# Two-branch attention on one core: another order at the end, one group turned by TensorE, and the first chunk's sums turned two slots later

## The chip, the cores and the metric

The kernel runs on one core of a Trainium2 chip. The core has TensorE (PE, matmuls into PSUM), ScalarE (ACT), VectorE (DVE), GpSimd (POOL) and SyncE (SP), which here only issues DMAs. Each engine works through its own queue in order, and semaphores make one wait for another. The metric is the device time of one execution in microseconds, the median of several.

## The reference

Two attention layers over 2048 tokens of 640 features, 32 heads of 20, whose outputs stand side by side. A is causal within chunks of 512 tokens and adds a linear memory of the chunks before; B is causal in a window of 256.

```python
# A, chunk s of 4 (L = 512)
logits = einsum('bhqd,bhkd->bhqk', qs, ks) * scale + mask      # causal in the chunk
a_dot = einsum('bhqk,bhkd->bhqd', softmax(logits), vs)
num = einsum('bhld,bhde->bhle', phi(qs), M)                    # phi(t) = t + 1 or exp(t)
den = einsum('bhld,bhd->bhl', phi(qs), z)[..., None] + 1e-06
outs.append(g * num / den + (1.0 - g) * a_dot)
M = M + einsum('bhld,bhle->bhde', phi(ks), vs); z = z + phi(ks).sum(l)
...
# B: mask (0 <= i - j < 256)
p = softmax(where(mask, q @ k.T * Dh ** -0.5, -1e9)); o = p @ v
...
return concatenate([o_A @ A_wo, o_B @ B_wo], axis=-1)
```

## The kernel before

**Phases and packs.** The work is cut into chunks of 512 tokens, and the eight phases run B0, A0, B1, A1, B2, A2, B3, A3. A phase has 8 groups g of 4 heads each (a `Unit`). Its scores come in packs: a pack is 512 columns of scores (keys on partitions, queries in the columns) for 4 heads, put together from one or two entries. A phase of A has 20 packs, B0 has 20, the other phases of B have 24. One pack is one slot (`self.slot`), and `body` writes out the order of all engines' instructions slot by slot. Within a slot it is: what is due in `after` for this slot (`at`), the pack's scores and exponentials (`scores`), what is due in `behind` (`at_end`), turns of outputs (`prefetch`), one group's weighted sums (`weigh`) if one is ready, what is due in `last_of`, and then projections, memory reads and output halves: in the first two phases from the fixed lists of `plan`, later as `pick` chooses them. Since every engine's queue is in order, the order of these calls is the order on each engine.

**One group's way.** `scores` (L492) puts the scores of two heads into each of two PSUM tiles `Sc` (three buffers), ScalarE takes exponentials into `pt` (L498), and GpSimd zeroes the masked triangles (L512, L518). Two slots after a group's last pack `weigh` multiplies `pt` by v into a PSUM tile `D` (L547); v carries a column of ones, so each head's sum comes with it. VectorE copies `D` to `oc`, a DMA on SyncE's queue turns it (L565), and some slots later `normalise` divides: a reciprocal (L596), a product into `o_tok` (L603) and, for A's later chunks, a sum with the memory's part (L612). Projections, sums and output halves all use the PSUM tile `D`, which has two buffers that are handed out in turn: whoever takes one waits until the reader of the tile before the last is done. TensorE waits there, with everything behind it in its queue.

**First chunk.** In chunk 0 two groups are turned together (`weigh_two`): the even group's sums go to the left half of a buffer (`omem` or `phiq`, taken in turn), the odd group's to the right half (L578), then one DMA turns both (L581), and `normalise` follows five and six slots later. In the same slots of B0 the projections of groups 4 to 6 go through DRAM: `proj_rest` writes rows of k and q (L276, `kdB`, `qdB`), and two slots later `spread` reads them back in the layout of the scores (L310, `kpB`, `qpB`, four DMAs each). The projections of A0 are written the same way (L290, `kdA`, `qdA`). All of these are on SyncE's queue. A DMA there that waits holds up those behind it.

**The end.** Phase A3 has no projections left. Its groups 0 to 5 are weighed in the loop, 6 and 7 in `tail`. Group 5 is weighed in the phase's slot 16; its division is due in slot 19, the last, after `last_turn` (L673, L676), which turns three of the five blocks of 128 features of `o_tok` by TensorE, and before the last pack's scores. For the last pack, GpSimd masks the first two heads (L505), and VectorE the others in `tail`, by a multiplication with `cmask` (L821). In `tail` the sums of group 6 and 7 are turned by TensorE (`turn_here`, L588), group 7 in two halves; blocks 3 and 4 are turned by `last_block` (L707) and copied by ScalarE (L838, L849); and `last_mm` (L681) multiplies by A's output weights, block by block, into PSUM tiles that `last_store` and the last lines write out.

Of the kernel before, what the change touches and what calls it, by code (L numbers as in the profile page):

```python
# [8 lines left out]
ALU = mybir.AluOpType  # L9
BF16 = mybir.dt.bfloat16  # L10
F32 = mybir.dt.float32

P = 128
# [7 lines left out]
NC = 4  # L21
CH = 512
CT = CH // P
# [59 lines left out]
class Kern:  # L83
# [400 lines left out]
    def scores(self, pk, last=False):  # L484
        nc = self.nc
        ps = [self.ps.tile([P, 2, CH], F32, name="Sc", bufs=3) for _ in range(2)]
        for (u, kt, off, q0, nq) in pk.entries:
            kp = self.kp[u.br, kt // CT]
            k0 = (kt % CT) * P
            for j in range(4):  # L490
                rows = slice(32 * j, 32 * j + DH)
                nc.tensor.matmul(ps[j // 2][:, j % 2, off * P:(off + nq) * P],  # L492
                                 lhsT=kp[rows, u.g, k0:k0 + P],
                                 rhs=self.qp[u.br][rows, u.g, q0 * P:(q0 + nq) * P],
                                 start=True, stop=True, tile_position=(32 * j, 0))
        pt = self.wk.tile([P, 4, CH], BF16, name="pt", bufs=6)
        for hp in range(2):
            nc.scalar.activation(out=pt[:, 2 * hp:2 * hp + 2, 0:pk.used],  # L498
                                 in_=ps[hp][:, :, 0:pk.used], func=ACT.Exp, scale=SCALE)
        for (u, kt, off, q0, nq) in pk.entries:  # L500
            loc = kt - u.c * CT
            if last:
                b = off + loc - q0
                blk = pt[:, 0:2, b * P:(b + 1) * P]
                nc.gpsimd.affine_select(out=blk, in_=blk, pattern=[[0, 2], [1, P]],  # L505
                                        compare_op=ALU.is_ge, fill=0.0, base=0,
                                        channel_multiplier=-1)
                self.open_masks.append(pt[:, 2:4, b * P:(b + 1) * P])
            elif 0 <= loc - q0 < nq:
                b = off + loc - q0  # L510
                blk = pt[:, :, b * P:(b + 1) * P]
                nc.gpsimd.affine_select(out=blk, in_=blk, pattern=[[0, 4], [1, P]],  # L512
                                        compare_op=ALU.is_ge, fill=0.0, base=0,
                                        channel_multiplier=-1)
            if u.br == "B" and 0 <= loc + WT - q0 < nq:
                b = off + loc + WT - q0
                blk = pt[:, :, b * P:(b + 1) * P]
                nc.gpsimd.affine_select(out=blk, in_=blk, pattern=[[0, 4], [-1, P]],  # L518
                                        compare_op=ALU.is_ge, fill=0.0, base=-1,
                                        channel_multiplier=1)  # L520
        for e in pk.entries:
            u = e[0]
            u.work.append((e, pt))
            u.left -= 1
            if u.left == 0:
                self.ready.append((self.slot + LAG, u))

    def weigh(self, u):
        nc = self.nc
        O = self.dtile([P, CH], F32)  # L530
        written = [False] * CT
        jobs = []
        for (_, kt, off, q0, nq), pt in u.work:
            runs = []
            for b in range(nq):
                w = written[q0 + b]
                if runs and runs[-1][2] == w:
                    runs[-1][1] += 1
                else:
                    runs.append([b, 1, w])  # L540
                written[q0 + b] = True
            jobs += [(kt, off + b, q0 + b, nb, pt) for b, nb, _ in runs]
        for n, (kt, off, q0, nq, pt) in enumerate(jobs):
            v = self.vt[u.br][(kt // CT) % 2 if u.br == "B" else 0]
            for j in range(4):
                v0 = VW * (4 * u.g + j)
                nc.tensor.matmul(O[32 * j:32 * j + 32, q0 * P:(q0 + nq) * P],  # L547
                                 lhsT=v[:, kt % CT, v0:v0 + 32],
                                 rhs=pt[:, j, off * P:(off + nq) * P],
                                 start=(n == 0), stop=(n == len(jobs) - 1),  # L550
                                 tile_position=(0, 32 * j))
        if u.c == 0:
            self.weigh_two(u, O)
            return
        oc = self.wk.tile([P, CH], BF16, name="oc", bufs=2)
        if self.closing:
            if u.g == G - 1:
                nc.scalar.copy(out=oc[:, 0:256], in_=O[:, 0:256])
                nc.scalar.copy(out=oc[:, 256:512], in_=O[:, 256:512])
            else:  # L560
                nc.vector.tensor_copy(out=oc[:], in_=O[:])
            return oc
        nc.vector.tensor_copy(out=oc[:], in_=O[:])  # L563
        tp = self.wk.tile([P, CT, P], BF16, name="ocT", bufs=4)
        nc.sync.dma_start_transpose(out=tp[:], in_=oc[:])  # L565
        late = 4 if u.br == "B" else 3 if u.c == NC - 1 else 5
        self.at(self.slot + late, lambda: self.normalise(u, tp[:]))

    def weigh_two(self, u, O):

        nc = self.nc
        i = u.g % 2
        if i == 0:
            t = self.io.tile([P, CT, D], BF16, name=("omem", "phiq")[u.g // 2 % 2], bufs=1)
            flat = t[:].rearrange("p t d -> p (t d)")
            self.two = [flat[:, k * 2 * CH:(k + 1) * 2 * CH] for k in range(2)] + [u]
        oc, tp, first = self.two
        nc.vector.tensor_copy(out=oc[:, i * CH:(i + 1) * CH], in_=O[:])  # L578
        if i:
            tp = tp.rearrange("p (b c) -> p b c", c=P)  # L580
            nc.sync.dma_start_transpose(out=tp, in_=oc)  # L581
            self.at(self.slot + 5, lambda: self.normalise(first, tp[:, 0:CT, :]))
            self.at(self.slot + 6, lambda: self.normalise(u, tp[:, CT:2 * CT, :]))

    def turn_here(self, u, oc, a=0, n=CT):
        tp = self.dtile([P, n, P], BF16)
# [112 lines left out]
        nc.sync.dma_start(out=self.out2d[r0:r0 + P, c0:c0 + D],  # L699
                          in_=ot[:].rearrange("p a b -> p (a b)"))  # L700

    def last_block(self, br, c, m, tiles, ps=None):

        if ps is None:
            ps = self.dtile([P, CT, P], BF16)
        for i in tiles:
            self.nc.tensor.transpose(out=ps[:, i, :],  # L707
                                     in_=self.o_tok[br, c][:, i, m * P:(m + 1) * P],
                                     identity=self.ident[:])
        return ps  # L710
# [101 lines left out]
    def tail(self, br, c):  # L812

        nc = self.nc
# [20 lines left out]
        ow = self.weigh(w)  # L835
        ps[2] = self.last_sc(2)
        self.last_mm(br, 2, 0, 3)
        nc.scalar.copy(out=self.oTs[:, 3, :, :], in_=self.last_block(br, c, 3, range(CT))[:])  # L838
        halves = [self.turn_here(w, ow, a, 2) for a in (0, 2)]
        halves[0]()  # L840
        halves[1]()
        for tt in range(3):
            self.last_mm(br, tt, 3, 4)
        tp = self.last_block(br, c, 4, (0, 1))
        end = [self.dtile([P, CH], F32)]
        self.last[CT - 1] = [end[0][:, 0:320]]
        self.last_mm(br, CT - 1, 0, 4, (0,))
        self.last_block(br, c, 4, (2, 3), tp)
        nc.scalar.copy(out=self.oTs[:, 4, :, :], in_=tp[:])  # L849
        for tt in range(3):  # L850
            self.last_mm(br, tt, 4, KT)
            self.last_store(br, c, tt, ps[tt], (nc.vector, nc.scalar)[tt % 2])
# [6 lines left out]
        for hf in range(2):  # L859
# [4 lines left out]
                out=self.out2d[r0:r0 + P, c0 + 320 * hf:c0 + 320 * hf + 320], in_=ot)  # L864
# [50 lines left out]
```

## Time and profile before

| | us |
|---|---|
| median of 3 runs | 368.64 (368.05 to 368.89) |
| the profiled execution | 368.28 |
| its span, first to last instruction | 366.2 |
| TensorE busy | 335.7 |
| ScalarE busy | 337.7 |
| GpSimd busy | 273.0 |
| VectorE busy | 260.6 |
| L498, exponentials, 344 of them | 321.9 |

The granted TensorE clock is 0.998 throughout. A row of a timeline has the start in microseconds from the span's start, the length, the engine (SPq is SyncE's queue, PEld the weight load), the line, the operation, what it writes and reads, the shape and how many are merged; in brackets stands how long the engine was idle before it, and what ended that. Consecutive exponentials overlap in the records; in the steady part one starts about every 0.9 us.

Where the engines stand in the two places concerned (busy us of the stretch):

| stretch, us | PE | DVE | ACT | POOL |
|---|---|---|---|---|
| 30 to 35 | 4.71 | 3.50 | 5.00 | 3.60 |
| 35 to 40 | 4.07 | 2.93 | 3.58 | 3.30 |
| 40 to 45 | 4.97 | 3.63 | 3.98 | 3.02 |
| 45 to 50 | 4.95 | 3.97 | 4.59 | 4.20 |
| 50 to 60 | 9.88 | 8.97 | 10.00 | 7.21 |

### The profile page before, as it was taken

The page shows a single profiled execution, that of the slowest core. Times are in us where ns is not written, and L with a number is a line of the kernel's source. Part 1 is how long each engine was busy: PE and PEld are TensorE (multiplying, and loading weights), DVE is VectorE, ACT ScalarE, POOL GpSimd, SP SyncE. Part 2 cuts the span into 40 slices and gives each one's busy share as a digit, 9 for nine tenths or more (in the row PEclk, how much of TensorE's full clock was granted, in tenths as well). Part 3 has the DMA queues.
Part 4 walks back from the last instruction along what each step waited for, and adds up shares of the span by engine and source line. Part 5 has one row for each costly group of instructions (what it writes and reads, how often), then busy time and mean ns, then how long its engine had stood idle before and what let it go on. Part 6 is the DMA issues. An engine that isn't in the chain of part 4 may idle for free.

```text
span 366.2 us, 10376 instructions
## 1 busy us (share of the span) xinstructions
PE 335.7 (92%) x3921; PEld 159.2 (43%) x3960; DVE 260.6 (71%) x554; ACT 337.7 (92%) x387; POOL 273.0 (75%) x436
## 2 busy tenths in 40 slices
PE   8999899999998989899979989979999999988994
PEld 4433444333534444344433445434544445444553
DVE  2466686766789697755689986775567877677583
ACT  2679799999999999999999999989999999999982
POOL 9675685555797877679888878758898878767850
PEclk9999999999999999999999999999999999999999
DMA  8974545676436788727675887636754767544732
GB/s 248 307 250 107 134 114 129 164 171 157 125 109 149 129 187 170 181 68 160 104 168 124 139 154 152 154 59 113 146 111 114 135 140 123 139 120 102 142 86 72
DMA packets 111842, 51.78 MB, mean 141 GB/s; under 512 B 81744, under 2 KB 111792, under 8 KB 111792
## 3 DMA queue, kind: packets, MB, share of 16 engines
q1 hardware_dynamic: 111648, 51.04, 61.6%
q8 instruction: 31, 0.51, 0.6%
q14 instruction: 19, 0.16, 0.1%
q10 hardware_dynamic: 144, 0.08, 0.1%
HBM read 16.88 MB, written 14.94 MB: 87 GB/s over the span
## 4 chain that ended last, share of the span: by engine, by line
PE 41%; ACT 26%; DVE 16%; issue 7%; DMA 6%; POOL 3%; SPq 1%; ACTq 0%; POOLq 0%; DVEq 0%
ACT pt L498 24%; PE D L286 11%; PE Sc L492 7%; PE D L346 6%; PE D L547 5%; PE D L638 4%; DVE qk L289 4%; PE D L255 3%; DMA ocT<-oc 2%; DVE oc L563 2%; DVE omem L478 2%; DMA oT<-otB 2%; POOL pt L512 1%; ACT pe L330 1%; DVE otA L603 1%
## 5 line engine op out<-in xcount | busy, mean ns | idle before, releaser
L498 ACT ACTIVATE pt<-Sc 128x1024 bf16<-128x1024 f32 (+1 forms) x344 | 321.9, 1096 | 13.6 <-PE Sc L492 10.3
L512 POOL TENSOR_SCALAR_AFFINE_SELECT pt<-pt 128x512 bf16<-128x512 bf16 x254 | 164.2, 657 | 77.6 <-ACT pt L498 77.0
L518 POOL TENSOR_SCALAR_AFFINE_SELECT pt<-pt 128x512 bf16<-128x512 bf16 x112 | 75.5, 689 | 2.5 <-ACT pt L498 2.2
L289 DVE CAST qk<-D 128x512 bf16<-128x512 f32 x70 | 48.1, 687 | 33.2 <-PE D L286 31.4
L492 PE MATMUL Sc<-qpB,kpB 20*128 20x256 bf16 (+2 forms) x704 | 45.4, 275 | 5.3 <-ACT pt L498 2.8
L563 DVE CAST oc<-D 128x512 bf16<-128x512 f32 x46 | 31.7, 688 | 16.7 <-PE D L547 16.4
L492 PE MATMUL Sc<-qpA,kpA 20*128 20x384 bf16 (+3 forms) x512 | 40.6, 300 | 2.1 <-ACT pt L498 1.5
L641 DVE CAST ot<-D 128x320 bf16<-128x320 f32 x56 | 27.3, 487 | 8.6 <-PE D L638 7.8
L638 PEld LDWEIGHTS <-oT 128*128 128x128 bf16 x280 | 24.9, 98 | 17.7 <-issue 7.0
L492 PEld LDWEIGHTS <-kpB 20*128 20x128 bf16 x704 | 14.5, 91 | 41.2 <-issue 40.0
L638 PE MATMUL D<-Bo,oT 128*128 128x320 bf16 x160 | 26.5, 300 | 1.5 <-DVE rm L475 0.9
L547 PE MATMUL D<-pt,vB 128*32 128x384 bf16 (+2 forms) x720 | 25.9, 275 | 1.6 <-DVE qk L289 1.6
L346 PE MATMUL D<-Av,xTA 128*128 128x320 bf16 x160 | 26.5, 300 | 0.7 <-DVE qk L289 0.6
L286 PE MATMUL D<-xTA,Ak 128*128 128x512 bf16 x90 | 24.3, 381 | 2.9 <-DVE oc L563 2.4
L346 PE MATMUL D<-Bv,xTB 128*128 128x320 bf16 x160 | 25.9, 300 | 0.2 <-DVE phiq L578 0.2
L286 PE MATMUL D<-xTA,Aq 128*128 128x512 bf16 x89 | 24.4, 381 | 1.8 <-DVE qk L289 0.7
L492 PEld LDWEIGHTS <-kpA 20*128 20x128 bf16 x512 | 12.5, 91 | 31.1 <-issue 28.8
L547 PE MATMUL D<-pt,vA 128*32 128x256 bf16 (+3 forms) x576 | 23.3, 287 | 0.3 <-DVE rm L475 0.3
L330 ACT ACTIVATE pe<-qk 128x512 bf16<-128x512 bf16 x30 | 22.0, 734 | 0.0
L286 PE MATMUL D<-xTB,Bk 128*128 128x512 bf16 x65 | 18.2, 380 | 3.0 <-DVE omem L478 2.0
L352 DVE CAST vB<-D 128x320 bf16<-128x320 f32 x32 | 15.5, 489 | 7.2 <-PE D L346 6.6
L638 PE MATMUL D<-Ao,oT 128*128 128x320 bf16 x120 | 19.9, 300 | 0.1
(107 smaller groups left out, 378.4 us busy)
## 6 DMA issues: line engine op xcount, KB each, us to landing
out_dram<-ot SPq DMA_DIRECT2D x31, 160.0 KB
kdA<-qk SPq DMA_DIRECT2D x20, 128.0 KB
qdA<-qk SPq DMA_DIRECT2D x20, 128.0 KB
kdB<-qk SPq DMA_DIRECT2D x17, 128.0 KB
qdB<-qk SPq DMA_DIRECT2D x17, 128.0 KB
kpB<-kdB SPq DMA_DIRECT2D x8, 160.0 KB
qpB<-qdB SPq DMA_DIRECT2D x8, 160.0 KB
kpA<-kdA SPq DMA_DIRECT2D x8, 160.0 KB
```

What stands on the lines that cost most here:

```text
L286: nc.tensor.matmul(ps[:], lhsT=self.w[br + which][:, kt, m * P:(m + 1) * P], rhs=self.xT[br][:, kt, :], start=(kt == 0), stop=(kt == KT - 1))
L289: nc.vector.tensor_copy(out=t[:], in_=ps[:])
L330: nc.scalar.activation(out=e[:], in_=t[:], func=ACT.Exp)
L346: nc.tensor.matmul(ps[:, 0:320], lhsT=self.xT[br][:, kt, tt * P:(tt + 1) * P], rhs=self.w[br + "v"][:, kt, hf * 320:(hf + 1) * 320], start ...
L492: nc.tensor.matmul(ps[j // 2][:, j % 2, off * P:(off + nq) * P], lhsT=kp[rows, u.g, k0:k0 + P], rhs=self.qp[u.br][rows, u.g, q0 * P:(q0 + ...
L498: nc.scalar.activation(out=pt[:, 2 * hp:2 * hp + 2, 0:pk.used], in_=ps[hp][:, :, 0:pk.used], func=ACT.Exp, scale=SCALE)
L512: nc.gpsimd.affine_select(out=blk, in_=blk, pattern=[[0, 4], [1, P]], compare_op=ALU.is_ge, fill=0.0, base=0, channel_multiplier=-1)
L518: nc.gpsimd.affine_select(out=blk, in_=blk, pattern=[[0, 4], [-1, P]], compare_op=ALU.is_ge, fill=0.0, base=-1, channel_multiplier=1)
L547: nc.tensor.matmul(O[32 * j:32 * j + 32, q0 * P:(q0 + nq) * P], lhsT=v[:, kt % CT, v0:v0 + 32], rhs=pt[:, j, off * P:(off + nq) * P], star ...
L563: nc.vector.tensor_copy(out=oc[:], in_=O[:])
L638: nc.tensor.matmul(ps[:, 0:320], lhsT=st["oT"][:, m, :], rhs=self.w[br + "o"][:, m, hf * 320:(hf + 1) * 320], start=(m == 0), stop=(m == K ...
L641: nc.vector.tensor_copy(out=st["ot"][:, hf * 320:(hf + 1) * 320], in_=ps[:, 0:320])
```

## The change

There are five edits.

1. In the last pack, the entry that begins at the last block of queries (`q0 < nq` does not hold for it, 3 against 1) has its second two heads masked by GpSimd too. VectorE keeps one multiplication of two.
2. Group 5 of A3 is no longer turned by DMA and divided three slots later. In the next slot, behind that slot's scores, TensorE turns it into a tile `D`, and VectorE divides it there and then.
3. The turn of the pairs (0, 1) and (2, 3) of B0 is issued two slots later, as the first thing of its slot, and their divisions come two slots later too.
4. In `tail`, block 3 is copied by VectorE and not by ScalarE, and group 7 is turned and divided in one go.
5. Block 4 is turned in one go, after the products of block 3 and before those of the last token tile, not half before and half after them.

```diff
@@ scores
-                self.open_masks.append(pt[:, 2:4, b * P:(b + 1) * P])
+                rest = pt[:, 2:4, b * P:(b + 1) * P]
+                if q0 < nq:
+                    self.open_masks.append(rest)
+                else:
+                    nc.gpsimd.affine_select(out=rest, in_=rest, pattern=[[0, 2], [1, P]],
+                                            compare_op=ALU.is_ge, fill=0.0, base=0,
+                                            channel_multiplier=-1)
@@ weigh
         nc.vector.tensor_copy(out=oc[:], in_=O[:])
+        if (u.br, u.c, u.g) == ("A", NC - 1, 5):
+            self.at_end(self.slot + 1, lambda: self.turn_here(u, oc)())
+            return
         tp = self.wk.tile([P, CT, P], BF16, name="ocT", bufs=4)
@@ weigh_two
-            nc.sync.dma_start_transpose(out=tp, in_=oc)
-            self.at(self.slot + 5, lambda: self.normalise(first, tp[:, 0:CT, :]))
-            self.at(self.slot + 6, lambda: self.normalise(u, tp[:, CT:2 * CT, :]))
+            wait = 2 if u.br == "B" and u.g < 4 else 0
+            if wait:
+                self.at(self.slot + wait, lambda: nc.sync.dma_start_transpose(out=tp, in_=oc))
+            else:
+                nc.sync.dma_start_transpose(out=tp, in_=oc)
+            self.at(self.slot + wait + 5, lambda: self.normalise(first, tp[:, 0:CT, :]))
+            self.at(self.slot + wait + 6, lambda: self.normalise(u, tp[:, CT:2 * CT, :]))
@@ last_block
-    def last_block(self, br, c, m, tiles, ps=None):
+    def last_block(self, br, c, m):
...
-        if ps is None:
-            ps = self.dtile([P, CT, P], BF16)
-        for i in tiles:
+        ps = self.dtile([P, CT, P], BF16)
+        for i in range(CT):
@@ tail
-        nc.scalar.copy(out=self.oTs[:, 3, :, :], in_=self.last_block(br, c, 3, range(CT))[:])
-        halves = [self.turn_here(w, ow, a, 2) for a in (0, 2)]
-        halves[0]()
-        halves[1]()
+        nc.vector.tensor_copy(out=self.oTs[:, 3, :, :], in_=self.last_block(br, c, 3)[:])
+        self.turn_here(w, ow)()
         for tt in range(3):
             self.last_mm(br, tt, 3, 4)
-        tp = self.last_block(br, c, 4, (0, 1))
+        nc.scalar.copy(out=self.oTs[:, 4, :, :], in_=self.last_block(br, c, 4)[:])
         end = [self.dtile([P, CH], F32)]
         self.last[CT - 1] = [end[0][:, 0:320]]
         self.last_mm(br, CT - 1, 0, 4, (0,))
-        self.last_block(br, c, 4, (2, 3), tp)
-        nc.scalar.copy(out=self.oTs[:, 4, :, :], in_=tp[:])
```

## The prediction

> **What bounds the kernel now.** I read the page first, then the timeline of the two places that the change touches, then the chain of waits.
>
> The page:
>
> ```profile
> PE 335.7 (92%) x3921; PEld 159.2 (43%) x3960; DVE 260.6 (71%) x554; ACT 337.7 (92%) x387; POOL 273.0 (75%) x436
> ```
>
> ScalarE's exponentials (L498) and TensorE share the bound. From 49 us to the end of the exponentials ScalarE has few gaps, so a microsecond won or lost before that stays won or lost to the end, unless ScalarE later waits for something else. Two places decide.
>
> The start, timeline (start, length, instruction, idle before and its releaser); SPq is SyncE's queue:
>
> ```profile
> 27.80 1.24 SPq L581 DMA_TRANSPOSE omem<-omem  x1
> 30.81 0.35 SPq L276 DMA_DIRECT2D kdB<-qk  x1
> 31.72 1.69 SPq L290 DMA_DIRECT2D kdA<-qk  x1
> 34.31 1.44 SPq L310 DMA_DIRECT2D kpB<-kdB  x4
> 35.85 1.43 SPq L310 DMA_DIRECT2D qpB<-qdB  x4
> 37.49 1.42 PE L492 MATMUL Sc<-qpB,kpB 20*128 20x256 bf16 x4 [0.57 <-DMA qpB<-qdB]
> 38.27 1.94 ACT L498 ACTIVATE pt<-Sc 128x1024 bf16<-128x1024 f32 x2 [1.43 <-PE Sc L492]
> ```
>
> The scores of pack 12 wait for qpB (0.57 us, and the four matmuls then take 1.42 us; the four before them, at 36.63, took 0.29). qpB is late because kpB, ahead of it on SyncE's queue, is late. That wait, in the same queue's list of waits (total, times, longest):
>
> ```profile
> SPq L310 <- DMA kdB<-qk: 3.2, 2, 2.4
> ```
>
> The longest, 2.4, is at 26.27; the other 0.8 is the wait from 33.41 to 34.31 for kdB's write, issued at 30.81, 3.4 us before. An instruction fetch falls into that time (DMA view of 31 to 35 us: one packet, 2.1% of 16 engines over 4 us, so 1.3 us on one engine; the packet itself runs from 31.83 to 33.15).
>
> The end, timeline:
>
> ```profile
> 348.80 0.85 PE L638 MATMUL D<-Bo,oT 128*128 128x320 bf16 x5
> 349.42 0.25 DVE L596 RECIPROCAL rr<-ocT 128x16 f32<-128x16 bf16 x1 [0.41 <-DMA ocT<-oc]
> 350.63 0.85 PE L638 MATMUL D<-Bo,oT 128*128 128x320 bf16 x5
> 350.98 1.03 DVE L641 CAST ot<-D 128x320 bf16<-128x320 f32 x2
> 353.07 0.24 DVE L596 RECIPROCAL rr<-ocT 128x16 f32<-128x16 bf16 x1
> 354.09 0.57 DVE L612 TENSOR_TENSOR otA<-otA,omem 128x320 bf16<-128x320 bf16 x1
> ```
>
> and the chain that ended last, in order of time:
>
> ```profile
> 351.52 0.50 DVE ot L641
> 352.07 0.49 PE D L673 x6
> 352.56 0.33 PE Sc L492 x8
> ...
> 356.37 0.92 PE Sc L681 x6
> ...
> 357.56 0.59 ACT pkt L838
> 358.19 0.27 PE D L588 x2
> ...
> 360.72 0.99 PE Sc L681 x6
> ```
>
> VectorE works without a break from 349.42 to 356.90, and its cast L641 releases the PSUM tile that the last block of turns (L673) needs. Those stand in TensorE's queue ahead of the last scores (L492 at 352.56). So every delay of L641 delays the last scores, and all behind them.
>
> **The change part by part.**
>
> *First chunk's sums two slots later, SyncE's queue (A).* Without the transposition at 27.80 to 29.04 the four qpB issues follow kpB's at 27.75. kdB's cast (DVE L273, 28.26 + 0.69) then lets kdB issue at 29.2 instead of 30.81 and qdB (cast 29.34 + 0.69) at 30.1; the transposition comes at 30.45 to 31.7, and kdA at 31.7 as before. kdB needs 3.4 us to land even at its present price: 32.6. What is late next is kdA's issue, held to 33.41 over the fetch, which TensorE's unchanged instructions start at the same time. So kpB starts at 33.45 to 33.6 in place of 34.31: 0.7 to 0.85 earlier, and the stall is shorter by as much. Bounds: the whole stall, 0.57 + 1.42 - 0.29 = 1.7 us; or a loss of 0.25, if kdA's pieces lie behind a transposition that the fetch has held up (33.15 + 64 packets of 22 ns, 1.4 us). I take **-0.8**. The second transposition (39.31) goes behind three writes and ahead of qpA's spread, which waited 1.5 us for its own write: nothing, as the A scores start only at 53.80; without that cover its 1.24 us would be lost.
>
> *The same sums, VectorE.* Each division is one L596 and one L603, 0.24 + 0.49 at 46.92 and 0.24 + 0.97 at 49.04. The first two leave slots 11 and 12, where TensorE waits for DMA, and go into 13 and 14, where TensorE has no idle time from 38.84 on: there two casts of v (41.93, 42.61), then the sums' cast L578 (43.72), come 0.6 to 1.0 later. The two PSUM tiles D let the sums L547 wait some 0.3 (42.77 to 43.06) and the projection at 45.00 a little more (**B +0.3**; bounds 0 and 0.4). The other two leave 16 and 17 for 18 and 19, where VectorE is busy without a break from 49.04 to 54.84. They bring 1.5 to 2.4 us; 0.3 is there at 49.91. The cast L289 at 54.16 then ends 0.7 to 2.1 later than 54.84, and the second v projection of slot 20 with it; it ended at 55.73, and ScalarE needs the scores behind it by 56.7, some 0.6 us of cover. **C +0.6**, between 0 and 1.3, nearer the middle as GpSimd's masks run beside it (52.74 to 56.08).
>
> In those rows L603 takes 0.49 with GpSimd idle for part of it and 0.97 with GpSimd at work throughout. [...]
>
> *The group turned by TensorE (D).* Group 5's four transposes stand behind the scores of slot 17, at 348.87; oc is ready at 348.44. They take 0.40 (L588 at 355.32) and fit before 350.31, when the next scores wait for ScalarE. The cost is VectorE's: reciprocal, product and sum now stand ahead of the two casts L641 instead of behind the copies L676. Duration: 0.26 + 0.49 + 0.33 with the gaps 1.15 (rows at 355.75, 356.04, 356.57, GpSimd idle), or 0.24 + 0.70 + 0.57 and gaps, 1.6 (rows at 353.07 on, GpSimd busy). Also a third tile goes round the two D buffers: the projection of 350.63 takes the buffer that the product reads, so it waits to some 351.9, ends at 352.8, and its cast at 353.3 to 353.5 where it was 352.02. The last scores come **D +1.35** later (1.1 to 1.6); ScalarE, which has its last exponential but two done by 353, idles. Taking the old division from in front of L561 (354.58) gives nothing on the path: TensorE reached the turn of 355.32 only at 355.28. The DMA transposition saved on SyncE (348.82) had nothing waiting but stores.
>
> *The last groups (E).* From the end of L547 (356.37) to the last row above takes 4.35 us now: 0.92, 0.24, 0.59 for the copy, then the half that waits for that copy's buffer (0.56), and so on. New: 0.92 + 0.24 + copy on VectorE 0.40 (L676: 1.11 for two of 768 columns, here 512; bounds 0.37 and ScalarE's 0.59) + reciprocal, product, sum in one go 0.26 + 0.49 + 0.33 + four transposes 0.24 + copy 0.59, and gaps of 0.03 to 0.05 each: 3.69. **E -0.65** (-0.45 to -0.7).
>
> *The late mask.* One multiplication (0.24) leaves VectorE, a third select (0.43) comes to GpSimd: it starts with the last exponential's end (354.92 now) and is done 0.43 later, before the last quarter of L547 (355.64 + 0.5). Nothing; without this cover 0.2.
>
> Sum: -0.8 + 0.3 + 0.6 + 1.35 - 0.65 = **+0.8**, on a span of 366.2 in an execution of 368.28: 369.1. The median of the runs, 368.64, lies 0.36 above that execution, so about **369.4**.
>
> **Rivals.**
> R1, faster: SyncE is not held at kdA, because the fetch falls on the transposition's tail, and the whole 1.7 us go; B and C small then (0.1), as ScalarE's waits there were TensorE's. -1.7 + 0.1 + 1.35 - 0.65 = -0.9: 367.7. For it: qdB's issue at 23.46 took 0.34 in spite of pending loads. Against: kdA's 1.69. It decides from the point where kpB issues before 33.
> R2, no change: VectorE's lateness in slots 13 to 20 is covered by the spare tile and ScalarE's 0.6 us: -0.8 + 0.1 + 0 + 1.35 - 0.65 = 0: 368.6. For it: VectorE has 1.8 us idle before 40.13. Against: no break from 49 on.
> R3, the early part turns round: kdA stays behind the transposition (+0.25), C at 1.3, B 0.3: +2.5: 371.1.
> R4, the last scores don't wait: group 5's division runs in the time that VectorE waits for L638, so D is at most 0.1 and the sum -0.45: 368.2. For it: the cast at 351.52 still waits for TensorE. Against: group 4's division ends at 351.06, and VectorE is in order. [...]
> R5, the later transposition changes nothing at the start (kpB waits as long for kdB): +1.6: 370.2.
>
> **How the numbers follow.** Forecast 0.44 (own range 368.8 to 370.0), R2 0.22, R1 0.12, R3 0.10, R4 0.07, R5 0.05. The range, 368.0 to 370.5, leaves out R1 and R3. 0.2%, 0.74 us, is about what can be told from no change. Slower by more, above 369.4: a bit over half of the forecast, R3, R5, 0.42. Faster by more, below 367.9: R1 and part of R4, 0.17. Within: 0.41.
>
> **What would show it.** A: kpB's second issue near 33.5, the wait before pack 12's second scores halved. B, C: ScalarE idle near 56 to 58 us, VectorE's L289 a microsecond behind its projection. D: L673 and the last L492 over a microsecond after the last but one exponential, which leaves a ScalarE gap before the last pack. E: L547's end to the last block of L681, 3.7 us. Wrong if no gap stands before the last pack, or if the start's stall is gone altogether.

## The result: 370.51 us, 1.0067 of the kernel before

| | kernel before | changed kernel |
|---|---|---|
| median of 20 runs each, taken side by side, us | 367.94 (366.56 to 369.41) | 370.51 (367.95 to 373.73) |
| ratio, 95% interval | | 1.0067 (1.0040 to 1.0094) |
| profiled execution, span, us | 366.2 | 370.1 |

The change makes the kernel slower by some 2.5 us (0.0067 of 367.94), three times the 0.8 that was forecast. 370.51 lies at the upper end of the range, 368.0 to 370.5, with some luck: the forecast was counted from a median of 368.64, and the kernel before came out at 367.94 this time. From 368.64 the ratio would have given 371.1. The changed kernel's times also spread wider than those of the kernel before.

The page of the changed kernel. The busy times are those of before within 1.3 us, so the 3.9 us of span are waits:

```profile
span 370.1 us, 10377 instructions
PE 335.6 (91%) x3925; PEld 158.6 (43%) x3964; DVE 259.7 (70%) x551; ACT 337.3 (91%) x386; POOL 274.3 (74%) x437
```

The start, timeline of the changed kernel:

```profile
29.55 0.35 SPq L276 DMA_DIRECT2D kdB<-qk  x1
31.79 0.53 SPq L290 DMA_DIRECT2D kdA<-qk  x1
32.42 1.47 SPq L310 DMA_DIRECT2D kpB<-kdB  x4
33.93 2.10 SPq L310 DMA_DIRECT2D qpB<-qdB  x4
36.92 1.94 ACT L498 ACTIVATE pt<-Sc 128x1024 bf16<-128x1024 f32 x2 [0.33 <-PE Sc L492]
...
53.83 0.84 PE L346 MATMUL D<-Av,xTA 128*128 128x320 bf16 x5 [0.74 <-DVE phiq L587]
54.57 1.20 SPq L337 DMA_TRANSPOSE pkt<-phik  x1
55.19 0.84 PE L346 MATMUL D<-Av,xTA 128*128 128x320 bf16 x5 [0.52 <-DVE qk L289]
56.48 11.11 ACT L498 ACTIVATE pt<-Sc 128x1024 bf16<-128x1024 f32 x12 [0.78 <-POOL pt L518]
```

kdB is issued 1.26 us earlier than before (30.81), kdA takes 0.53 and not 1.69, and pack 12's exponentials begin 1.35 earlier (38.27 before). Of this, 0.25 is no work of the change: pack 8, ahead of the place concerned, already starts at 29.50 against 29.75. By pack 21, at 56.48 against 56.70, only 0.22 is left: nothing of the win. On the way TensorE waits twice for VectorE between v projections of slot 20, 0.74 and 0.52, where before it ran ten matmuls without a break. The row at 56.48 names GpSimd as the last release (its mask ended at 56.46), but the scores themselves began only at 55.96; the exponentials follow 0.52 behind, about as for the last pack below (357.07 to 357.56).

Then comes what no term of the forecast has. Same view, further on:

```profile
64.00 2.95 SPq L107 DMA_TRANSPOSE xTB<-in_B_x_dram  x1
70.51 2.31 PE L286 MATMUL D<-xTB,Bk 128*128 128x512 bf16 x5 [3.40 <-DMA xTB<-in_B_x_dram]
73.49 3.77 ACT L498 ACTIVATE pt<-Sc 128x1024 bf16<-128x1024 f32 x4 [3.56 <-PE Sc L492]
```

TensorE waits 3.40 us for the load of the next chunk's x for branch B, and ScalarE 3.56 for TensorE. The same two instructions in the kernel before:

```profile
62.61 2.56 SPq L107 DMA_TRANSPOSE xTB<-in_B_x_dram  x1
67.62 1.24 PE L286 MATMUL D<-xTB,Bk 128*128 128x512 bf16 x5 [0.22 <-DVE omem L578]
```

There the load was complete by 67.2, and the first weight load had waited 0.21 us for it: just in time. In the changed kernel 15 of the load's 16 parts are done by 68.94, and the last one comes at 70.47; an instruction fetch (one packet, from 68.24, 1.15 us) falls into that time. Then TensorE runs at a lower clock. The changed kernel in stretches (us; busy of PE, PEld, DVE, ACT, POOL with counts; granted clock; DMA share; GB/s):

```profile
60.00:66.00 6.00, 5.46 (x71) 2.47 (x70) 2.37 (x4) 6.00 (x8) 3.26 (x7) 1.00 0.63 137
66.00:70.00 4.00, 1.11 (x13) 0.47 (x11) 2.97 (x8) 3.92 (x5) 1.74 (x3) 1.00 0.77 172
70.00:74.00 4.00, 3.40 (x10) 0.97 (x12) 0.69 (x1) 0.51 (x1) 1.22 (x2) 0.57 0.28 84
```

The kernel before does 41 matmuls in 70 to 74 us at clock 1.00; this one does 10 at 0.57:

```profile
70.00:74.00 4.00, 3.95 (x41) 1.62 (x40) 2.22 (x4) 4.00 (x6) 1.86 (x3) 1.00 0.63 147
```

The five projections after the wait, which took 1.24 us before, take 2.31. In this trace 3.40 us of idle time come first, then a clock of 0.57 over 4 us (0.50 for 3.41 of them), then 1.00 again (74 to 80 us).

The end, timeline of the changed kernel:

```profile
354.66 0.49 DVE L616 TENSOR_TENSOR otA<-D,rr 128x320 bf16<-128x320 bf16 x1
355.21 0.85 PE L651 MATMUL D<-Bo,oT 128*128 128x320 bf16 x5 [1.11 <-DVE otA L616]
357.07 0.40 PE L492 MATMUL Sc<-qpA,kpA 20*128 20x384 bf16 x8
357.56 1.94 ACT L498 ACTIVATE pt<-Sc 128x1024 bf16<-128x1024 f32 x2 [1.16 <-PE Sc L492]
360.01 0.73 PE L553 MATMUL D<-pt,vA 128*32 128x256 bf16 x20
...
364.53 0.99 PE L694 MATMUL Sc<-Ao,pkt 128*128 128x320 bf16 x6
```

Group 5's product (L616) reads a tile D that the next projection (L651) waits for, 1.11 us, and the last pack's exponentials wait 1.16: that pack shifts by 1.18 against the packs ahead of it. From the end of the sums L553 (360.74) to the last block of products (364.53) takes 3.79 us, where before it took 4.35.

What the clock of the whole execution tells: 7 of 18 runs of the changed kernel (two disturbed ones, 373.68 and 373.73, are left out) have a mean granted clock of 0.998 or more, and their median is 368.28; the other 11 lie below that clock, with a median of 371.78. Of the 92 runs of the kernel before that stood beside the experiments, 55 reach 0.998, with a median of 367.35, and 37 do not, with 369.10. So there are two losses: some 0.9 us in executions without a dip of the clock (368.28 against 367.35, on several chips, hence rough), and dips that cost more (3.5 us against 1.75) and perhaps come oftener (11 of 18 against 37 of 92, too few to be sure). A mean does not tell where a dip lies. One stretch of 3.41 us at 0.50 makes a mean of 0.995, wherever it is; the 0.998 of the kernel before's profile is such a mean too, 1.00 up to 364.6 us and 0.50 behind. Three other executions that were profiled, of early_only, best3 and before_x_late below, have a mean of 0.994 or 0.995 and no stall at 70 us: their clock is at 0.50 for 3.41 us from 334.7, 335.0 and 333.0. In before_x_late:

```profile
329.50:333.00 3.50, 2.41 (x39) 1.32 (x40) 2.92 (x11) 3.50 (x5) 2.92 (x6) 0.99 0.50 121
333.00:336.40 3.40, 3.40 (x29) 1.35 (x18) 1.75 (x4) 2.05 (x3) 3.12 (x6) 0.50 0.21 43
```

The packs there lose 1.3 to 1.5 us, which is near the 1.75 of the kernel before's dips. In the 5 us ahead of these dips TensorE was never idle for more than 0.81 us. In the profiled execution of the kernel before it does the same work (2.41 us busy in 331 to 334.5), and the clock stays at 1.00. So a dip can come without a long wait; why it comes in some executions and not in others is not shown.

### The profile page after: what moved, and what is told of

Its sections match the earlier page's. It is cut to its first block, busy times and chain, and to the rows that moved or that the text cites. A ratio compares the mean times of both kernels' runs of the same rounds, so it can differ in the third digit from the quotient of the medians.

```text
span 370.1 us, 10377 instructions
## 1 busy us (share of the span) xinstructions
PE 335.6 (91%) x3925; PEld 158.6 (43%) x3964; DVE 259.7 (70%) x551; ACT 337.3 (91%) x386; POOL 274.3 (74%) x437
## 4 chain that ended last, share of the span: by engine, by line
PE 35%; ACT 26%; DVE 17%; DMA 9%; issue 7%; POOL 4%; SPq 0%; ACTq 0%; POOLq 0%; DVEq 0%
ACT pt L498 25%; PE D L286 10%; PE Sc L492 6%; PE D L346 4%; PE D L651 4%; PE D L553 4%; DMA ocT<-oc 3%; DVE qk L289 3%; PE D L255 3%; POOL pt L518 2%; DVE oc L569 2%; DMA xTB<-in_B_x_dram 2%; DVE omem L478 2%; DVE otA L616 1%; DMA oT<-otB 1%
## 5 line engine op out<-in xcount | busy, mean ns | idle before, releaser
L289 DVE CAST qk<-D 128x512 bf16<-128x512 f32 x70 | 48.1, 687 | 38.2 <-PE D L286 36.0
L492 PE MATMUL Sc<-qpA,kpA 20*128 20x384 bf16 (+3 forms) x512 | 39.4, 302 | 1.7 <-ACT pt L498 1.0
L654 DVE CAST ot<-D 128x320 bf16<-128x320 f32 x56 | 27.2, 486 | 8.7 <-PE D L651 8.0
L651 PEld LDWEIGHTS <-oT 128*128 128x128 bf16 x280 | 24.9, 98 | 18.7 <-issue 7.0
L651 PE MATMUL D<-Bo,oT 128*128 128x320 bf16 x160 | 26.5, 300 | 2.6 <-DVE otA L616 1.1
L553 PE MATMUL D<-pt,vB 128*32 128x384 bf16 (+2 forms) x720 | 25.9, 275 | 1.7 <-DVE qk L289 1.6
L286 PE MATMUL D<-xTB,Bk 128*128 128x512 bf16 x65 | 19.3, 399 | 6.2 <-DMA xTB<-in_B_x_dram 3.4
L553 PE MATMUL D<-pt,vA 128*32 128x256 bf16 (+3 forms) x576 | 23.3, 287 | 0.3 <-DVE rm L475 0.3
L651 PE MATMUL D<-Ao,oT 128*128 128x320 bf16 x120 | 19.9, 300 | 0.1
```

What stands on the lines that cost most here:

```text
L286: nc.tensor.matmul(ps[:], lhsT=self.w[br + which][:, kt, m * P:(m + 1) * P], rhs=self.xT[br][:, kt, :], start=(kt == 0), stop=(kt == KT - 1))
L289: nc.vector.tensor_copy(out=t[:], in_=ps[:])
L651: nc.tensor.matmul(ps[:, 0:320], lhsT=st["oT"][:, m, :], rhs=self.w[br + "o"][:, m, hf * 320:(hf + 1) * 320], start=(m == 0), stop=(m == K ...
L654: nc.vector.tensor_copy(out=st["ot"][:, hf * 320:(hf + 1) * 320], in_=ps[:, 0:320])
```

## The experiments

"Ratio" is to the kernel before in runs taken side by side. "Held" means that SyncE's issue of kdA took over 1.5 us and not about 0.5.

**Which half: early_only** is the kernel before with edit 3 alone, **end_only** the changed kernel without edit 3.

```diff
@@ early_only, weigh_two
+            wait = 2 if u.br == "B" and u.g < 4 else 0
...
-            self.at(self.slot + 5, lambda: self.normalise(first, tp[:, 0:CT, :]))
+            self.at(self.slot + wait + 5, lambda: self.normalise(first, tp[:, 0:CT, :]))
...
@@ end_only, weigh_two
-            wait = 2 if u.br == "B" and u.g < 4 else 0
...
-            self.at(self.slot + wait + 5, lambda: self.normalise(first, tp[:, 0:CT, :]))
+            self.at(self.slot + 5, lambda: self.normalise(first, tp[:, 0:CT, :]))
...
```

> The kernel before with edit 3 alone (pairs turned and divided two slots later). Theory: the exponentials of pack 12 start 1.1 to 1.4 us earlier than before, and by pack 21 nothing of that is left, since the two divisions in slots 18 and 19 make VectorE late. Then either the load of chunk 1's x lands in time (execution within 0.5 us of before) or its last part falls behind an instruction fetch and some 3.5 us are lost at its first reader, L286; executions spread over 367.5 to 372, median +0.5 to +2.5 us. Rival (the spread and the mean loss come from the end): median within 0.5 us, spread as narrow as before's.

> The kernel before with edits 1, 2, 4 and 5 (the end), without edit 3. Theory: last pack's scores 1.2 us later, from the end of the last L547 to the last block of products 0.65 us less: +0.5 us (+0.4 to +0.8), with before's narrow spread of 366.5 to 369.5. Rival (the loss of 2.5 us in the median comes from the end): +2 us or more.

early_only: 369.94 against 368.61, ratio 1.0036 (1.0006 to 1.0066). end_only: 368.55 against 368.61, ratio 1.0012 (0.9978 to 1.0046). The medians put most of the loss into the early half, but the two intervals overlap. In early_only's profile pack 12 begins 0.57 earlier than before, half of what was expected, as its whole stream was 0.52 late at pack 8; pack 21 is 0.38 late, the reader of the load waits 0.89, and the dip at 334.7 costs another 1.3. In end_only the last pack shifts by 1.18 and the end then wins 0.70 back: +0.5 net in its profile. Its times did not keep to the narrow spread that was expected: the slowest is 371.82, without edit 3. But this kernel, without edit 3, also begins pack 12 early, by 1.31 us: what edit 3 was to win at the start was there without it.

**The early half taken apart: early_dma_only** moves only the transpositions, **div_late_only** only the divisions, both on the kernel before.

```diff
@@ early_dma_only, weigh_two
-            nc.sync.dma_start_transpose(out=tp, in_=oc)
+            wait = 2 if u.br == "B" and u.g < 4 else 0
+            if wait:
+                self.at(self.slot + wait, lambda: nc.sync.dma_start_transpose(out=tp, in_=oc))
+            else:
+                nc.sync.dma_start_transpose(out=tp, in_=oc)
@@ div_late_only, weigh_two
+            wait = 2 if u.br == "B" and u.g < 4 else 0
             nc.sync.dma_start_transpose(out=tp, in_=oc)
-            self.at(self.slot + 5, lambda: self.normalise(first, tp[:, 0:CT, :]))
-            self.at(self.slot + 6, lambda: self.normalise(u, tp[:, CT:2 * CT, :]))
+            self.at(self.slot + wait + 5, lambda: self.normalise(first, tp[:, 0:CT, :]))
+            self.at(self.slot + wait + 6, lambda: self.normalise(u, tp[:, CT:2 * CT, :]))
```

> As early_only, but the divisions stay where they were (5 and 6 slots after the sums), only the DMA turn is issued two slots later. Theory: the 1.1 to 1.4 us won at pack 12 are still there at pack 21, since VectorE's slots 18 and 19 are as before; a run without the collision at the load of x is 1 us faster than before, one with it 2 to 3 us slower. Rival (the win is lost to something else than the moved divisions, such as TensorE's own load): no more than 0.3 us are left at pack 21, as in early_only.

> The kernel before with only the divisions of the pairs (0, 1) and (2, 3) two slots later; the DMA turns stay where they were. Theory (VectorE's lateness in slots 18 to 20 costs, and through the exponentials' memory part phik, which VectorE makes, also holds SyncE's queue): from pack 13 to pack 21 ScalarE loses 1.2 to 1.5 us against end_no_turn, the load of chunk 1's x is issued near 63.5 us and not 61 to 62, its first reader waits in part of the executions, median +1 to +2.5 us. Rival (the DMA's new place in the queue is what makes the load late): no loss at pack 21, load at 61 to 62, +0.3 us or less.

early_dma_only: 368.78 against 368.61, ratio 1.0015 (0.9990 to 1.0040), no difference. div_late_only: 369.28 against 367.33, ratio 1.0061 (1.0028 to 1.0095): the moved divisions alone cost about as much as the whole change. Its timeline shows how:

```profile
51.69 0.96 DVE L604 TENSOR_TENSOR otB<-phiq,rr 128x320 bf16<-128x320 bf16 x1
53.81 0.83 DVE L333 TENSOR_TENSOR phik<-phik,pe 128x512 bf16<-128x512 bf16 x1
53.94 0.84 PE L346 MATMUL D<-Av,xTA 128*128 128x320 bf16 x5 [0.74 <-DVE phiq L578]
54.67 1.20 SPq L337 DMA_TRANSPOSE pkt<-phik  x1
55.30 0.84 PE L346 MATMUL D<-Av,xTA 128*128 128x320 bf16 x5 [0.52 <-DVE qk L289]
62.95 2.63 SPq L107 DMA_TRANSPOSE xTB<-in_B_x_dram  x1
67.64 1.25 PE L286 MATMUL D<-xTB,Bk 128*128 128x512 bf16 x5 [0.42 <-DMA xTB<-in_B_x_dram]
```

and early_dma_only, same view:

```profile
52.70 1.53 PE L346 MATMUL D<-Av,xTA 128*128 128x320 bf16 x10
52.77 1.20 SPq L337 DMA_TRANSPOSE pkt<-phik  x1
```

With the divisions in slots 18 and 19, VectorE reaches the product L333 later, so the turn of its result (L337) goes out at 54.67 and not at 52.77. All DMAs behind it on SyncE's queue are later as well; the load of x is the one that counts, 62.95 against 61.04 in early_dma_only. Here it came 0.42 us too late, without a dip of the clock before 366 us. The ten times of div_late_only show what else can happen: five lie between 367.9 and 368.3, and five between 370.3 and 372.9.

**The start without the moved divisions: end_dma_late** is edits 1, 4 and 5 with early_dma_only's edit.

> Edits 1, 4 and 5 and the DMA half of edit 3 (turns two slots later, divisions in their old slots). Theory (kdB's earlier write only pays in executions whose fetch falls between 31 and 32.5 us, few of them): same as end_no_turn within 0.15%, ratio 0.9960 to 0.9985. Rival (the start is held in most executions, and the profile of before was typical): 1 us better than end_no_turn, ratio 0.9935 to 0.9955.

367.63 against 368.19, ratio 0.9998 (0.9965 to 1.0030). The same edits without the DMA's move (end_no_turn, below) have ratios of 0.9967 and 0.9971. The intervals overlap, and 0.9998 lies outside the ranges of the theory and of the rival. So no gain of the earlier kdB is seen. Why follows from the executions that were profiled:

| execution | fetch starts, us | kdA issued at, for, us | pack 12's exponential, us |
|---|---|---|---|
| before | 31.83 | 31.72, 1.69 | 38.27 |
| end_no_turn_again | 31.8 to 32.1 | 31.91, 1.95 | 38.69 |
| end_no_turn | 32.96 | 31.94, 0.40 | 37.13 |
| end_only | 34.03 | 32.01, 0.40 | 36.96 |
| best3 (transpositions later) | 32.1 to 32.4 | 32.33, 1.51 | 37.97 |
| end_dma_late (transpositions later) | 31.5 to 31.8 | 31.78, 1.55 | 37.51 |
| changed kernel (transpositions later) | 33.36 | 31.79, 0.53 | 36.92 |

The instruction fetch falls at another time in each execution. Where it started within 0.2 us of kdA's issue, that issue was held until 0.3 to 0.4 us after the fetch's end; this was so in 4 of the 14 executions profiled, two of seven with the transpositions moved and two of seven without. In the ten others the fetch starts 0.9 to 2.0 us behind the issue, and kdA takes 0.39 to 0.53. There pack 12 starts near 37.0 in either order (36.91 to 37.17 in eight; 37.38 in after_x_early and 37.70 in early_only, whose whole streams are later). Counted from the start of pack 8, which lies between 29.40 and 30.27, pack 12 comes after:

| | transpositions moved | not moved |
|---|---|---|
| not held, five each, us | 7.42 to 7.43 | 7.42 to 7.65 |
| held, two each, us | 7.72 and 7.98 | 8.52 and 8.93 |

So the move wins 0.88 in the mean where the issue is held, and 0.12 where it is not.

**The load's lateness, from three sides.** **after_x_early** is the changed kernel with the load of x at the end of slot 19's list, **after_reader_late** the changed kernel with the load's first reader (`Bkq`) one step later, **before_x_late** the kernel before with the load one step later.

```diff
@@ after_x_early, plan
-             [q[7]], [Aq[2]], [Ak[2]], [Ak[3]], [Aq[3]]],
-            [vA[0][0:2], [vA[0][2]] + xB, [Aq[4]], [vA[0][3]], [vA[1][0]],
+             [q[7]], [Aq[2]], [Ak[2]], [Ak[3]], [Aq[3]] + xB],
+            [vA[0][0:2], [vA[0][2]], [Aq[4]], [vA[0][3]], [vA[1][0]],
@@ after_reader_late, plan
-             [Ak[4]], [vA[1][1]], [Bkq[0]], [Bkq[1]], [vA[1][2]],
+             [Ak[4]], [vA[1][1]], [vA[1][2]], [Bkq[0]], [Bkq[1]],
@@ before_x_late, plan
-            [vA[0][0:2], [vA[0][2]] + xB, [Aq[4]], [vA[0][3]], [vA[1][0]],
+            [vA[0][0:2], [vA[0][2]], [Aq[4]] + xB, [vA[0][3]], [vA[1][0]],
```

> The changed kernel with the load of chunk 1's x (B) issued at the end of slot 19 and not in slot 21. Theory: the load is complete before the fetch near 68 us, L286 doesn't wait, the clock stays at 1.0 in 70 to 74 us, and the spread of executions falls to some 2 us: +0.5 us against before (0 to +1). Rival (VectorE's lateness after slot 20 is what stalls L286): the stall of 3 to 4 us and the spread stay, +2 us or more.

> The changed kernel with the first two projections that read chunk 1's x (B) one slot later, and a projection of v (A) in the place of the first. Theory (TensorE idles for the late x, then runs at half clock): most of the stall of 3 to 4 us near 70 us goes, the granted clock there stays near 1, the median is +0.5 to +1.3 us against before and the slowest runs are no more than 2 us above the fastest. Rival (the queue's lateness itself, at the division of groups 6 and 7, is what stalls): the stall stays, +2 us or more.

> The kernel before with the load of chunk 1's x issued one slot later (22). Theory: about 1.8 us later load, L286 waits 1 to 3 us for it, TensorE's clock falls below 0.8 in the 4 us after a wait of 3 us or more, +1 to +4 us. Rival (the load has room): +0.3 us or less.

after_x_early, with four runs, is far slower, 375.38 against 368.61, ratio 1.0186 (1.0129 to 1.0242). This cure fell. Its timeline:

```profile
56.95 2.86 SPq L107 DMA_TRANSPOSE xTB<-in_B_x_dram  x1
64.88 1.23 SPq L594 DMA_TRANSPOSE phiq<-phiq  x1
68.37 0.25 DVE L609 RECIPROCAL rr<-phiq 128x16 f32<-128x16 bf16 x1 [2.56 <-DMA phiq<-phiq]
70.44 1.26 PE L286 MATMUL D<-xTB,Bk 128*128 128x512 bf16 x5 [2.88 <-DVE omem L587]
```

The load takes 2.86 us of SyncE's queue at 56.95, ahead of A0's spreads and the turn of groups 6 and 7. That turn comes late, a division waits 2.56 us for it, the sums' cast stands behind the division, and TensorE waits 2.88 for the cast at the same place as before. So the load is not the only thing that can be late: the whole queue is full there, and what is put forward puts something else back.

after_reader_late: 369.48 against 368.45, ratio 1.0025 (0.9997 to 1.0053), against the changed kernel's 1.0067. Its row of the windows for the same stretch:

```profile
70.00:74.00 4.00, 3.98 (x40) 1.55 (x41) 2.04 (x4) 3.93 (x6) 1.92 (x4) 1.00 0.43 110
```

40 matmuls at clock 1.00, as in the kernel before: in the profiled execution the stall is gone, its reader starting at 70.02 after 0.34 us of idle. The load was no better there: its last sixteenth came at 69.97, the others by 68.40. The later reader covered it. The times' upper end falls from 373.73 to 371.77, still 3.0 above the fastest where at most 2 was expected. The two ratios' intervals overlap, so the size of this gain is not shown, but the place is.

before_x_late: 367.94 against 367.33, ratio 1.0019 (0.9987 to 1.0051). In its profile the load goes out at 61.98 and the reader waits 0.65. That execution was not held at kdA, so its load was earlier than the held kernel before's in spite of the edit, and the run does not test what it was for: inconclusive. Its loss in the profile is the dip at 333.0.

**The end: end_no_turn** is the changed kernel without edits 2 and 3, **end_turn_late** end_only with group 5's turn behind the last pack's scores.

```diff
@@ end_no_turn, weigh
-        if (u.br, u.c, u.g) == ("A", NC - 1, 5):
-            self.at_end(self.slot + 1, lambda: self.turn_here(u, oc)())
-            return
...
@@ end_turn_late, weigh
-            self.at_end(self.slot + 1, lambda: self.turn_here(u, oc)())
+            self.at_end(self.slot + 3, lambda: self.turn_here(u, oc)())
```

> The kernel before with edits 1, 4 and 5 alone: the end without the group turned by TensorE, and without edit 3. Theory (group 5's division ahead of the two casts costs 1.2 us, the last groups' order wins 0.65): the last pack's scores come as before, the end of the last L547 to the last block of products 3.7 us instead of 4.35: 0.6 to 0.7 us faster than before (ratio 0.998). Rival (the order of the last groups is worth nothing by itself, it only takes back what the turn lost): 0.0.

> As end_only, but group 5 is turned and divided behind the last pack's scores and not behind those of slot 17, so its division stands behind the casts and copies on VectorE. Theory (order on VectorE and the two PSUM tiles cost 1.2 us): the last scores as early as before relative to the exponentials ahead, no gap of 1.2 us before the last pack; then 0.4 us more on TensorE for the turn; in all -0.2 us against before. Rival (it is the turn on TensorE itself that costs): the 1.2 us stay, somewhere before the end of the last L547.

> The same kernel as end_no_turn, in more rounds. Theory: 0.65 us less at the end, ratio 0.9965 to 0.9985. Rival (the first look was luck): ratio 0.999 to 1.001.

end_no_turn: 367.31 against 368.45, ratio 0.9967 (0.9937 to 0.9996). The same kernel once more: 366.63 against 367.33, ratio 0.9971 (0.9952 to 0.9990). The kernel before is beaten by 0.3%, with both intervals below 1, and this is the best one found. Its end:

```profile
351.13 0.40 PE L492 MATMUL Sc<-qpA,kpA 20*128 20x384 bf16 x8
354.08 0.73 PE L553 MATMUL D<-pt,vA 128*32 128x256 bf16 x20
358.59 0.99 PE L687 MATMUL Sc<-Ao,pkt 128*128 128x320 bf16 x6
```

From the sums' end (354.81) to the last block, 3.78 us, as in the changed kernel, and no gap ahead of the last pack. end_turn_late (a single run, 366.17, span 364.5) has the turn by TensorE but behind the last scores:

```profile
351.09 0.40 PE L492 MATMUL Sc<-qpA,kpA 20*128 20x384 bf16 x8
351.42 0.40 PE L597 MATMUL D<-ident,oc 128*128 128x128 bf16 x4
```

The last exponential stands 1.41 us earlier than in the kernel before, and so do those some 40 ahead of it: nothing is lost there. Behind the last scores it does cost something: from these to the sums L553 it takes 3.33 us (351.09 to 354.42), against 2.95 in end_no_turn. One execution has no median, so its time, 366.17, proves little. What costs the 1.2 us ahead of the last scores is thus not the turn by TensorE, but its reader ahead of the casts L654 and the third tile in the round of the two buffers; the two were not told apart.

The second profile of end_no_turn was one that was held:

```profile
31.91 1.95 SPq L290 DMA_DIRECT2D kdA<-qk  x1
34.71 1.44 SPq L310 DMA_DIRECT2D kpB<-kdB  x4
38.69 1.94 ACT L498 ACTIVATE pt<-Sc 128x1024 bf16<-128x1024 f32 x2 [1.84 <-PE Sc L492]
```

and its DMA view of 31.8 to 32.1 us has the fetch (packets, MB, share of 16 engines):

```profile
q8 instruction: 1, 0.02, 35.3%
```

The code and the order are the same as in end_no_turn's first profile, where kdA took 0.40 and pack 12 began 1.56 earlier. So the hold cost 1.56 at pack 12 in this pair. By pack 20 the two are 3.47 apart (56.89 against 53.42): in the held one the granted clock was 0.50 from 40.4 us on, for 3.41 us. The kernel before, held without such a dip, is 1.47 behind end_no_turn at pack 20 (54.90).

**All that seemed good in one: best3**, end_no_turn with early_dma_only's edit and the later reader.

> Edits 1, 4 and 5, edit 3 with the divisions left in their old slots, and the first readers of chunk 1's x one slot later. Theory: 0.65 us from the end and, in executions where the fetch would have hit kdB's write, up to 1.3 us from the start, with less of the stall near 70 us: 0.5 to 1.5 us faster than before. Rival (the win at the start is absorbed later, as in the profiled run of early_dma_only near 140 us): 0.3 to 0.7 us faster.

368.49 (366.35 to 369.28) against 368.45, ratio 0.9979 (0.9949 to 1.0010): the medians are equal, and the interval includes 1, so it is not seen to be better than end_no_turn alone. Its profiled execution was held at kdA and has the dip at 335.0.

## Why the prediction was right and where it was wrong

The direction and the signs of the parts B to E were right; the size was short, 0.8 against 2.5 us. About half of the shortfall is the win of part A, which most executions do not have: without it the forecast's own sum is 1.6. The rest lies in the load of x and in dips of the clock, which had no term, and is explained only in part.

**A, -0.8 forecast.** This step failed: "kdA's issue, held to 33.41 over the fetch, which TensorE's unchanged instructions start at the same time". The fetch does not start at the same time. It moved between 31.6 and 34.0 us over the executions, and with it the hold. That the fetch is TensorE's was the author's estimate; no view shows whose it is. The kernel before was read from an execution that was held; ten of the 14 profiled were not, and there is then next to nothing to win (0.12). Within held executions the forecast's mechanism seems right, and its size too: 0.88 from pack 8 to pack 12, but these are four executions of four kernels. R1's condition (kpB before 33) and the sign "the start's stall is gone altogether" both came true in the changed kernel's profile, and the time was not R1's: the stall's absence was no work of the change.

**B and C, +0.3 and +0.6.** The mechanism was right: TensorE waits for VectorE at the v projections of slot 20. The starts of the exponentials tell the two apart. From pack 20 to pack 21 it takes 2.76 us in all five executions with the divisions moved and 1.81 in all nine without: C is +0.95, within its bounds but half as much again as the 0.6 that was taken. From pack 13 to pack 20 it takes 13.72 to 14.14 in the five and 13.67 in the others (14.39 in the one with the dip at 40.4): B is +0.05 to +0.47, 0.2 in the mean. The term was mis-sized, not its parts. The two moved products L603 took 0.49 and 0.96, the two rows whose mean the forecast had used. The cast L289 ended 1.48 later against pack 20 than before (55.14 and 53.72 here, 54.84 and 54.90 before), near the middle of the forecast 0.7 to 2.1; less the 0.6 of cover that makes 0.9.

**What had no term.** C ended at ScalarE: "VectorE late, the second v projection late". What else waits for VectorE there was not followed: the product L333, whose turn stands on SyncE's queue ahead of the load of x. That queue in the changed kernel, with next to no time free from the turn to the load at 64.00:

```profile
54.57 1.20 SPq L337 DMA_TRANSPOSE pkt<-phik  x1
55.89 0.50 SPq L290 DMA_DIRECT2D qdA<-qk  x1
56.50 3.10 SPq L310 DMA_DIRECT2D kpA<-kdA  x4
59.64 1.21 SPq L337 DMA_TRANSPOSE pkt<-phik  x1
60.90 1.66 SPq L310 DMA_DIRECT2D qpA<-qdA  x4
62.66 1.23 SPq L594 DMA_TRANSPOSE phiq<-phiq  x1
```

So eleven DMAs later a delay of the turn is still a delay of the load. But not all of the load's lateness comes from there. Of the four issues of kpA, the first took 1.41 us in this execution, over a fetch that runs from 56.33 to 57.51; in the 13 others it took 0.29 to 0.31. From the turn to the load it is 9.4 us here and 8.2 to 8.45 in the eleven others with the load at its old place. div_late_only, with its turn at 54.67, issues the load 1.05 earlier, and its reader waits 0.42; early_only's waits 0.89. These waits of 0.4 to 0.9 are what the moved divisions bring. With the 3.40 of the changed kernel's profile there were two fetches more: the one that held kpA's first issue (1.41 us), and the one at 68.24, during which the last part came 1.53 behind the rest. Behind the idle time the clock was 0.50 for 3.41 us. Together this took 3.6 us in the profiled execution (from 0.2 ahead of the profile before at pack 21 to 3.4 to 3.6 behind at pack 28). It is the largest part of that execution's loss. By the clocks 11 of 18 runs have a dip of some size; whether the others have it at this place is not known. early_only, whose first half is the changed kernel's, has its dip at 334.7 us.

**D, +1.35.** Right: 1.18 in the changed kernel and 1.18 in end_only, with the waits where they were forecast. The forecast was near the middle of its bounds; the product took 0.49, the price of the quiet rows, though GpSimd was at work throughout (from 354.64 to 356.00); what sets that price is not shown. R4 (the last scores don't wait) fell.

**E, -0.65.** Right: 4.35 became 3.79 where 3.69 was forecast, and from the last pack's exponentials to the end of the span 0.7 is won (0.70 in end_only, 0.71 in the changed kernel). The late mask cost nothing that shows.

**R2, R3, R5.** R2 (VectorE's lateness covered) fell with C. R3's +2.5 is nearest to what was measured, but by another way: kdA was not behind a held transposition, and pack 12 was early. R5, which got the least chance, 0.05, has the mechanism of most executions: its premise, that the later transposition changes nothing at the start, is what the unheld ones show, and its +1.6 is near what B to E measured (0.2 + 0.95 + 1.2 - 0.7 = 1.65, without the load of x).

**Open.** The parts come to some 1.65, the median's loss is 2.5, and in the runs without a dip some 0.9 shows: held executions in the kernel before explain some of the last, how much is not settled. How much of the rest is the load's stall and how much dips elsewhere, and how often the stall falls in with a fetch, is open too, since only one execution of each kernel, two of end_no_turn, is profiled. It is not known what lowers the clock near 334 us in some executions, nor why early_dma_only, 1.5 us ahead up to pack 61 in its profile, lost 1.4 of it between 137 and 150 us. The halves' ratios (1.0036 and 1.0012) come to 1.0048, below 1.0067 but within the intervals.

## What to carry to other kernels

Before a stall is priced, ask whether it belongs to the kernel or to the one execution that was profiled: a wait that overlaps an instruction fetch is suspect (here kdA's issue was held in 4 of 14 executions), and a second profile tells, or that of a nearly equal kernel. The same holds for a loss after the change: a low mean clock does not say where the time went. When work is moved later on an engine, follow everything that this engine releases, the DMA queue above all, down to the next load that lands just in time. In the profiled execution 3.6 us were lost there, with two fetches in the way; in div_late_only's, 0.42. Group 5's turn by TensorE in a PSUM tile cost, with its reader, 1.18 us ahead of the last scores; behind them it cost some 0.4 (end_turn_late, one execution), and left to the DMA (end_no_turn) neither.

## What the runs showed of the hardware

In four of 14 executions one 16 KB instruction fetch (in the kernel before 31 of them move 0.51 MB) of 1.2 to 1.7 us held an issue on SyncE's queue to 1.5 to 1.95 us in place of 0.4 to 0.5; in each the fetch started within 0.2 us of the issue, and the issue ended 0.3 to 0.4 us after the fetch. In two executions (the changed kernel and after_reader_late) the last sixteenth of a load came 1.53 and 1.57 us after the rest while a fetch ran. In early_only it did not, though a fetch ran there too (from 67.86, all parts by 68.56), so which fetch delays a load is not shown. Between two executions of one kernel, end_no_turn unheld and held, pack 12's exponentials began 1.56 us apart (37.13 and 38.69).

The granted clock fell to 0.50 for 3.41 us not only after 3.40 us of idle time. It did so too after stretches of 3.4 us in which TensorE was busy for 2.1 to 2.4 us (before_x_late, early_only, best3 and the second execution of end_no_turn), and in the kernel before it did not after the same work.
